# Cutting the warm-up matmuls at the head of an SSM-plus-dense kernel into chunks, two of them released by VectorE's layernorm sums

## The chip, the cores and the metric

The kernel runs on one core of one Trainium2 chip. The metric is the device time in microseconds (us). The profile follows one execution; its span (first to last instruction) is about 1.4 us shorter than the time that is counted. Engines: PE is TensorE, PEld its weight loads, DVE VectorE, ACT ScalarE, POOL GpSimd, SP SyncE.

## The reference, cut to what matters

```python
xn = _layernorm(x)                              # x: 1 x 2048 x 1024, bf16
out = x + ssm(xn, Lambda, B, C, log_dt, Dskip) + mish(xn @ w1 + b1) @ w2
# ssm: Bu = xn @ B_bar; a scan over the 2048 positions; y = 2 Re(h @ C) + xn * Dskip
```

The kernel takes the 2048 positions in four blocks of 512. A block does the first dense product, the SSM projection, the scan on VectorE, and a tail that adds the second dense product and the output projection in PSUM (the memory, in banks, that the matmuls here write). All of it needs xn transposed. For the first block nothing is there to hide that behind: this stretch, from the start to the first matmul on real weights, is the *head*.

## The kernel before

A helper records every operation with the tiles it reads and writes, and works out from them what it must wait for. An operation that writes a bank waits for that bank's last writer, also if that was on the same engine. The head:

```python
def keep_busy(n):                         # n matmuls of the identity with itself, result unused
    for i in range(n):
        PE.mm(lambda e: e.matmul(ps[:, 3, 0:P], lhsT=ident[:], rhs=ident[:], start=True, stop=True),
              reads=[b_ident], writes=[b_ps[3]], first=i == 0, last=i == n - 1)

keep_busy(44)
aop(... AF.Sqrt ...)                      # ScalarE: loads its table early (at 2.43 us, 1.28 us long)
PE.op(lambda e: e.transpose(ps16(2)[:, 0:NST], st[:, :], ident[0:NST, 0:NST]), ...)   # parameters
keep_busy(12)
for q in range(2):                        # layernorm of rows 0..255, 128 at a time
    first_sums_v(q, 0); first_sums_v(q, 1); first_var_v(q)      # VectorE -> mv[q]
    first_sqrt(q)                                               # ScalarE
first_apply(0)                            # VectorE: xn[0]
first_transpose(0)                        # TensorE: 8 transposes
keep_busy(4)
first_apply(1); first_transpose(1)
keep_busy(4)
first_copy(0, VE, 0, 4); first_copy(1, VE, 0, 4)                # PSUM -> xnT
first_copy(0, AC, 4, NK); first_copy(1, AC, 4, NK)
... # layernorm of rows 256..511
for f in range(NSPLIT):
    first_half(f, 0)                      # the first matmuls on real weights
```

The kernel gives each engine its operations in the order in which they stand here. The identity matmuls compute nothing that is used: they are there so that TensorE's clock is full when the real matmuls begin.

## Time and profile before

| | us |
|---|---|
| first three runs | 624.6, 622.09, 622.07 |
| span of the profiled execution | 620.41 |
| first matmul on real weights starts | 8.76 |
| from there to the end | 611.65 |
| full clock granted (clock record) | 6.50 |

The page of the kernel before, its busy shares and the chain that ended last by engine:

```profile
PE 613.4 (99%) x2905; PEld 287.6 (46%) x2961; DVE 465.6 (75%) x687; ACT 244.7 (39%) x158; POOL 49.9 (8%) x47
...
PE 96%; ACT 2%; DVE 1%; issue 1%; POOL 0%; DVEq 0%; POOLq 0%
```

TensorE bounds the kernel. The change touches only the head, so there the question is what holds up the first real matmul. The chain of waits of the first 24 us (start in us, length in us, what):

```profile
1.42 4.87 PE ps L462 x44
6.29 0.15 PE ps L467
6.44 0.82 PE ps L462 x12
7.26 0.45 PE ps L383 x8
7.71 0.22 PE ps L462 x4
7.93 0.24 PE ps L383 x4
8.17 0.02 issue
8.19 0.42 DVE xnT L396
8.62 0.13 DVE par L486
8.75 0.02 issue
8.76 2.78 PE ps L502 x24
```

L462 is the identity matmuls, L467 the parameter transpose, L383 the transposes of xn, L502 the real matmuls. The identity matmuls are *on* the chain: TensorE gets through them only a little after VectorE has the first xn ready. That is in the timeline (start, length, instruction), two lines from VectorE and one from TensorE:

```profile
6.04 0.21 DVE L351 BATCH_NORM_AGGREGATE mv<-stats 128x2 f32<-128x12 f32 x1
6.31 0.55 DVE L371 TENSOR_SCALAR xn<-xx,mv,rs 128x1024 bf16<-128x1024 bf16 x1
...
7.10 0.61 PE L383 MATMUL ps<-ident,xn 128*128 128x128 bf16 x8
```

xn is ready at 6.86 us, and the first transpose starts at 7.10.

The clock can be counted. These are windows of the same profile (stretch, its length, busy time of PE and the matmuls that began in it, granted clock, DMA share, GB/s):

```profile
5.00:6.00 1.00, 1.00 (x13) 1.00 1.14 343
7.00:8.00 1.00, 1.00 (x22) 1.00 0.98 309
```

The busy time is the same and the count isn't: start to start it is 106.7 ns at first and 55.8 ns later. (The column of the granted clock shows 1.00 in both, since there is no record before the first grant; the spacing has to be read instead.) The clock record of this trace grants 1.00 from 6.50 us, 5.1 us after TensorE's first matmul, for 614.399 us, and 0.50 after that, behind the last instruction. Below, W is the moment of full clock, and *half clock* is the state in which identity matmuls start 106.7 ns apart.

### The profile page before, as it was taken

The page shows a single profiled execution, that of the slowest core. Times are in us where ns is not written, and L with a number is a line of the kernel's source. Part 1 is how long each engine was busy: PE and PEld are TensorE (multiplying, and loading weights), DVE is VectorE, ACT ScalarE, POOL GpSimd, SP SyncE. Part 2 cuts the span into 40 slices and gives each one's busy share as a digit, 9 for nine tenths or more (in the row PEclk, how much of TensorE's full clock was granted, in tenths as well). Part 3 has the DMA queues.
Part 4 walks back from the last instruction along what each step waited for, and adds up shares of the span by engine and source line. Part 5 has one row for each costly group of instructions (what it writes and reads, how often), then busy time and mean ns, then how long its engine had stood idle before and what let it go on. Part 6 is the DMA issues. An engine that isn't in the chain of part 4 may idle for free.

```text
span 620.4 us, 7332 instructions
## 1 busy us (share of the span) xinstructions
PE 613.4 (99%) x2905; PEld 287.6 (46%) x2961; DVE 465.6 (75%) x687; ACT 244.7 (39%) x158; POOL 49.9 (8%) x47
## 2 busy tenths in 40 slices
PE   8999999999999999999999999999999999999998
PEld 8544444444444444444444444444444444444443
DVE  6899999999467599998147659999624856999603
ACT  5679995441079940000009992000001999000000
POOL 1998000000100000000010000000000000000000
PEclk9999999999999999999999999999999999999999
DMA  9999967740464301763065420285204542033001
GB/s 261 244 292 277 204 132 206 202 136 0 157 182 141 132 1 36 220 186 103 17 189 165 140 100 1 92 215 163 75 35 136 167 139 69 1 128 111 1 0 69
DMA packets 124332, 79.41 MB, mean 128 GB/s; under 512 B 48906, under 2 KB 106762, under 8 KB 124298
## 3 DMA queue, kind: packets, MB, share of 16 engines
q1 hardware_dynamic: 120800, 71.58, 42.4%
q10 hardware_dynamic: 2538, 4.21, 1.9%
q0 software_dynamic: 960, 3.15, 1.6%
q8 instruction: 24, 0.39, 0.3%
q14 instruction: 10, 0.08, 0.0%
HBM read 63.19 MB, written 4.19 MB: 109 GB/s over the span
## 4 chain that ended last, share of the span: by engine, by line
PE 96%; ACT 2%; DVE 1%; issue 1%; POOL 0%; DVEq 0%; POOLq 0%
PE ps L721 49%; PE ps L644 26%; PE ps L664 18%; PE ps L502 2%; PE ps L462 1%; ACT act L624 1%; ACT act L622 1%; ACT act L623 1%; DVE hb L651 0%; DVE act L629 0%; PE ps L383 0%; ACT L623 0%; DVE xx L436 0%; DVE xx L758 0%; DVE mt L434 0%
## 5 line engine op out<-in xcount | busy, mean ns | idle before, releaser
L721 PE MATMUL ps<-ring,act 128*128 128x512 bf16 x880 | 193.2, 379 | 0.8
L644 PE MATMUL ps<-xnT,ring 128*128 128x512 bf16 x832 | 182.7, 379 | 0.8
L622 ACT ACTIVATE act<-hb 128x3584 bf16<-128x3584 bf16 x16 | 50.9, 3183 | 244.2 <-DVE hb L651 243.7
L721 PEld LDWEIGHTS ps<-ring,act 128*128 128x128 bf16 x896 | 87.6, 98 | 105.8 <-DVE mt L669 0.3
L644 PEld LDWEIGHTS ps<-xnT,ring 128*128 128x128 bf16 x848 | 83.0, 98 | 99.8
L651 DVE TENSOR_SCALAR hb<-ps,par 128x512 bf16<-128x512 f32 x112 | 82.7, 747 | 55.1 <-PE ps L644 53.8
L664 PE MATMUL ps<-xnT,BT 128*128 128x512 bf16 x500 | 110.5, 379 | 0.6
L721 PE MATMUL ps<-CT,hT 128*128 128x512 bf16 x500 | 110.5, 379 | 0.6
L669 DVE TENSOR_TENSOR mt<-ps,tab 128x1024 bf16<-128x1024 f32 x64 | 75.3, 1219 | 13.3 <-PE ps L664 11.7
L664 PEld LDWEIGHTS ps<-xnT,BT 128*128 128x128 bf16 x512 | 50.1, 98 | 60.4
L721 PEld LDWEIGHTS ps<-CT,hT 128*128 128x128 bf16 x512 | 50.1, 98 | 60.4
L758 DVE TENSOR_TENSOR xx<-ps,xx 128x1024 bf16<-128x1024 f32 (+1 forms) x17 | 19.5, 1160 | 70.2 <-PE ps L721 70.1
L687 DVE TENSOR_TENSOR_SCAN hT<-cs,qi,hT 128x512 bf16<-128x512 f32 x48 | 58.9, 1268 | 0.0
L624 ACT ACTIVATE act<-act 128x3584 bf16<-128x3584 bf16 x16 | 51.0, 3190 | 0.2
L623 ACT ACTIVATE act<-act 128x3584 bf16<-128x3584 bf16 x16 | 51.0, 3190 | 0.2
L692 DVE TENSOR_TENSOR mt<-hT,tab 128x1024 bf16<-128x1024 bf16 x64 | 41.4, 688 | 1.1
L629 DVE TENSOR_TENSOR act<-act,hb 128x3584 bf16<-128x3584 bf16 x16 | 32.3, 2018 | 1.3 <-ACT act L624 1.3
L287 POOL DMA_DIRECT2D xx<-in_A_x_dram x12 | 6.7, 559 | 253.1 <-DVE xx L758 248.6
L598 ACT ACTIVATE ct<-CT,cs 128x512 f32<-128x512 bf16 x16 | 11.5, 718 | 28.8 <-DVE CT L600 24.5
L623 ACT ACT_TABLE_LOAD x16 | 20.5, 1283 | 0.3
L624 ACT ACT_TABLE_LOAD x16 | 20.5, 1283 | 0.3
L687 DVE TENSOR_TENSOR_SCAN hT<-cs,hT 128x512 bf16<-128x512 f32 x16 | 18.7, 1208 | 0.0
(78 smaller groups left out, 277.2 us busy)
## 6 DMA issues: line engine op xcount, KB each, us to landing
ring<-in_B_w_dram SPq DMA_DIRECT2D x112, 512.0 KB, 3.9
out_dram<-xx ACTq DMA_DIRECT2D x15, 256.0 KB, 2.1
xx<-in_A_x_dram POOLq DMA_DIRECT2D x12, 256.0 KB, 4.5
xx<-in_A_x_dram SPq DMA_DIRECT2D x3, 256.0 KB, 4.8
xx<-in_A_x_dram SPq DMA_DIRECT2D x2, 128.0 KB, 2.2
dsk<-in_A_Dskip_dram SPq DMA_DIRECT2D x1, 256.0 KB, 7.0
out_dram<-xx ACTq DMA_DIRECT2D x2, 128.0 KB, 1.7
xnT<-xn SPq DMA_TRANSPOSE x12, 4.5
```

Source lines behind the costliest of these rows:

```text
L622: aop(lambda e: e.activation(a, hs, AF.Exp), reads=[b_hb[g % 2]], writes=[b_act[g]])
L623: aop(lambda e: e.activation(a, a, AF.Ln, bias=1.0), reads=[b_act[g]], writes=[b_act[g]])
L624: aop(lambda e: e.activation(a, a, AF.Tanh), reads=[b_act[g]], writes=[b_act[g]])
L629: vop(lambda e: e.tensor_tensor(a, a, hs, op=ALU.mult), reads=[b_act[g], b_hb[g % 2]], writes=[b_act[g]])
L644: PE.mm(lambda e, k=k: e.matmul(ps[:, bank, :], lhsT=wt[:, k, fi * P:(fi + 1) * P], rhs=xnT[:, k, :], start=k == 0, stop=k == NK - 1), rea ...
L651: vop(lambda e: e.tensor_scalar(hb[:, hs, :], ps[:, bank, :], b1(f), None, op0=ALU.add), reads=[b_ps[bank], b_par], writes=[b_hbf[hs]])
L664: PE.mm(lambda e, j=j, ci=ci, k=k, bank=bank: e.matmul(ps[:, bank + ci, :], lhsT=BT[:, ci, j, k, :], rhs=xnT[:, k, :], start=k == 0, stop= ...
L669: vop(lambda e, s=s, u=u, j=j: e.tensor_tensor(mt[:, s, :, :], u, tab[:, s, j, :].unsqueeze(1).to_broadcast([P, 2, TB]), op=ALU.mult), rea ...
L687: vop(lambda e, ci=ci, init=init: e.tensor_tensor_scan(out=hT[:, ci, j, :], data0=cj("r", j).to_broadcast([P, TB]), data1=hT[:, ci, j, :], ...
L692: vop(lambda e, s=s: e.tensor_tensor(mt[:, s, :, :], hT[:, :, j, :], tab[:, s, j, :].unsqueeze(1).to_broadcast([P, 2, TB]), op=ALU.mult), ...
L721: PE.mm(lambda e: e.matmul(ps[:, u, :], lhsT=lhsT, rhs=rhs, start=st_, stop=last), reads=reads, writes=[b_ps[u]], first=st_, last=last)
L758: vop(lambda e: e.tensor_tensor(xr, src, xr, op=ALU.add), reads=b_src + [b_x], writes=[b_x])
```

## The change

Its intent is that TensorE has work in every part of the head: the identity matmuls come in chunks, two of which are released by VectorE's finished sums.

```diff
-    def keep_busy(n):
+    def keep_busy(n, until=()):
         for i in range(n):
             PE.mm(lambda e: e.matmul(ps[:, 3, 0:P], lhsT=ident[:], rhs=ident[:], start=True, stop=True),
-                  reads=[b_ident], writes=[b_ps[3]], first=i == 0, last=i == n - 1)
-
-    keep_busy(44)
+                  reads=[b_ident, *until] if i == 0 else [b_ident], writes=[b_ps[3]], first=i == 0, last=i == n - 1)
+
+    keep_busy(30)
     aop(...)
-    PE.op(... transpose of the parameters ...)
-    keep_busy(12)
     for q in range(2):
         first_sums_v(q, 0)
         first_sums_v(q, 1)
         first_var_v(q)
         first_sqrt(q)
+        keep_busy(20 - 6 * q, until=[b_mv[q]])
+    PE.op(... transpose of the parameters ...)
     first_apply(0)
     first_transpose(0)
-    keep_busy(4)
+    keep_busy(3)
     first_apply(1)
     first_transpose(1)
-    keep_busy(4)
+    keep_busy(5)
```

Ahead of the first transpose of xn that makes 64 identity matmuls in three chunks (30, 20, 14) instead of 56 in two. The order on every other engine is the same.

More of the change, by code (lines that the diff above doesn't have):

```diff
@@ L457, in smalls @@
             reads=[b_cs[in0]], writes=[b_cs[out_]])
-    def keep_busy(n):
+    def keep_busy(n, until=()):
         for i in range(n):
             PE.mm(lambda e: e.matmul(ps[:, 3, 0:P], lhsT=ident[:], rhs=ident[:], start=True, stop=True),
-                  reads=[b_ident], writes=[b_ps[3]], first=i == 0, last=i == n - 1)
-    keep_busy(44)
+                  reads=[b_ident, *until] if i == 0 else [b_ident], writes=[b_ps[3]], first=i == 0, last=i == n - 1)
+    keep_busy(30)
     aop(lambda e: e.activation(rs[:, :, 3], kon[:, 2:3].to_broadcast([P, NQ]), AF.Sqrt), reads=[b_kon], writes=b_rs)
-    PE.op(lambda e: e.transpose(ps16(2)[:, 0:NST], st[:, :], ident[0:NST, 0:NST]),
-          reads=[b_st, b_ident], writes=[b_ps[2]])
-    keep_busy(12)
     for q in range(2):
@@ L474, in build_kernel @@
         first_sqrt(q)
+        keep_busy(20 - 6 * q, until=[b_mv[q]])
+    PE.op(lambda e: e.transpose(ps16(2)[:, 0:NST], st[:, :], ident[0:NST, 0:NST]),
+          reads=[b_st, b_ident], writes=[b_ps[2]])
     first_apply(0)
     first_transpose(0)
-    keep_busy(4)
+    keep_busy(3)
     first_apply(1)
     first_transpose(1)
-    keep_busy(4)
+    keep_busy(5)
     first_copy(0, VE, 0, 4)
```

## The prediction

> **What bounds the kernel.** TensorE: the page gives PE 99% of the span, and the chain that ended last is 96% PE. Only the head (0 to 8.8 us) changes. There PE runs only identity matmuls, one small transpose and the first layernorm's transposes. The chain over the first 24 us goes: 44 identity matmuls (4.87 us), small transpose, 12 identity matmuls, 8 transposes, 4 identity matmuls, 4 transposes, VectorE's copy of xnT (0.42), then the first real matmuls at 8.76 us. After that the waits of PE show only 0.2 us, so what the head gains or loses should reach the end one for one.
>
> **The clock.** In the trace the identity matmuls start 106.7 ns apart up to 6.4 us and 55.8 ns apart after it; the clock record says full speed from 6.50 us. [...]PE started at 1.41 us, full clock came 5.1 us later. So the moment of full clock (W) should vary from run to run[...]. I suspect that in the 624.6 run it came late[...]; the other two (622.07, 622.09) had it early.
>
> **What the change does.** Ahead of the first data transpose, 44+12 identity matmuls become 30+20+14, 8 more; the small transpose moves behind them. Each chunk writes the same bank, so it waits for the last one to end: in the trace a chunk follows that end by 0.09 us, a bubble of about 0.25 us; there is one more. The releases cost little: VectorE's first sums end at 4.69 us, the second at 6.25 (timeline); 30 cold matmuls end at 4.79, so chunk two starts at about 4.9 us, released as much by its own engine. The later chunks (4 and 4 to 3 and 5) are worth 0.06 us. VectorE's and ScalarE's order doesn't change.
>
> **Sum.** First xn is ready at 6.86 us, first transpose before at 7.10. After, with full clock at 6.5 us: chunk two's last matmul starts at 6.72, chunk three runs 7.03 to 7.8, first transpose 7.87, second group 8.49 (7.77 before), first real matmul about 9.5 instead of 8.76: +0.7 us. [...]The change buys dense PE work[...], and the 624.6 kind of run should vanish. The usual run gets slightly slower, the rare bad one better.
>
> Predicted median 622.6 us, 80% range 621.8 to 623.9; faster by over 2%: 0.005, within 2%: 0.99, slower: 0.005.
>
> **What would show it.** Right: first real matmul at 8.9 to 9.8 us; chunk three ends after xn0 is ready, so that the first data transpose waits on PE's own order; no PE idle over 0.3 us from 1.4 us to the transposes; everything after the same, shifted. Wrong: first real matmul at or before 8.76 us; chunk two or three waiting visibly for VectorE; a later wait that absorbs the shift.
>
> **What would make it wrong.** [...] If the 624.6 run has another cause (DMA, for one), after shows such runs too. [...]

The marked cuts took out what no trace of this case shows: the range expected for W, the reason supposed for a late clock, and what was built on these. From the sum they took the term for W at 8.2 us and that for W near 5 us. What is left of it came to +0.7 us at W = 6.5 us (first real matmul at about 9.5 us instead of 8.76); the forecast of 622.6 us was made with the cut terms. "Cold" means at half clock.

## The result, and the profile after

| | before | after |
|---|---|---|
| median of the two kernels' runs beside each other (6 each) | 622.26 | 622.75 |
| lowest, highest | 622.07, 624.6 | 622.11, 623.12 |
| span of the profiled execution | 620.41 | 621.11 |
| first transpose of xn starts | 7.10 | 7.83 |
| first real matmul starts | 8.76 | 9.45 |
| from there to the end | 611.65 | 611.66 |

The ratio of after to before is 1.0002 (95% interval 0.9986 to 1.0017): the same. A ratio is the mean time of one kernel's fast runs over that of the other's of the same rounds, so it isn't quite the ratio of the medians. Here the one run of 624.6 lifts the mean of before.

The chain of waits of the kernel after, first 24 us:

```profile
1.42 3.39 PE ps L462 x30
4.81 0.14 issue
4.95 1.75 PE ps L462 x20
6.69 0.14 issue
6.83 0.94 PE ps L462 x14
7.77 0.13 PE ps L473
7.90 0.55 PE ps L383 x8
...
9.45 2.78 PE ps L502 x24
```

(L473 is now the parameter transpose.) The head is still TensorE's own order, and longer. There are two "issue" pieces of 0.14 us that before had not: a chunk that waits for the chunk ahead of it. What the weight loads of the second and the third chunk waited for, and xn, from the timeline:

```profile
4.92 1.59 PEld L462 LDWEIGHTS ps<-ident 128*128 128x128 bf16 x20 [0.39 <-DVE mv L351]
...
6.31 0.55 DVE L371 TENSOR_SCALAR xn<-xx,mv,rs 128x1024 bf16<-128x1024 bf16 x1
6.80 0.80 PEld L462 LDWEIGHTS ps<-ident 128*128 128x128 bf16 x14 [0.29 <-issue]
...
7.83 0.62 PE L383 MATMUL ps<-ident,xn 128*128 128x128 bf16 x8
```

The profile puts the first wait down to VectorE's sums, but those ended at 4.72 us, while the last matmul of the first chunk ended at 4.80: both ended within 0.1 us of each other, and who was last is a matter of modelled ends. xn is ready at 6.86 us as before, and TensorE comes to it 0.97 us later. Everything behind the first real matmul takes 611.66 us, as before (611.65), so the head's 0.69 us reaches the end whole.

In this execution the spacing turns from 106.7 to 55.8 ns at about 5.9 us. (The trace has no clock record in this execution, though the spacing shows the change.) So the two profiles do not have the same W, and the difference of 0.69 us is not yet the cost of the change at equal clock.

### The profile page after: what moved, and what is told of

Same layout as the page of the kernel before. It is cut to its first block, busy times and chain, and to the rows that moved or that the text cites. A ratio compares the mean times of both kernels' runs of the same rounds, so it can differ in the third digit from the quotient of the medians.

```text
span 621.1 us, 7406 instructions
## 1 busy us (share of the span) xinstructions
PE 616.8 (99%) x2969; PEld 287.8 (46%) x2969; DVE 465.7 (75%) x687; ACT 244.8 (39%) x158; POOL 49.9 (8%) x47
## 4 chain that ended last, share of the span: by engine, by line
PE 99%; DVE 0%; POOL 0%; issue 0%; POOLq 0%
PE ps L721 49%; PE ps L644 29%; PE ps L664 18%; PE ps L502 2%; PE ps L462 1%; PE ps L383 0%; DVE xx L758 0%; DVE xnT L396 0%; POOL ident L330 0%; POOL ident L329 0%; DVE par L486 0%; PE ps L473 0%; POOL kon L333 0%; POOLq L844 0%
```

## The experiments

Theory: the head's time is TensorE's own order, that is the number of identity matmuls, the bubbles between chunks, and W, which varies from run to run. The prediction also supposed that the kernel's few runs near 624.6 are runs in which full clock came late. Rivals: VectorE's release or the place of the parameter transpose costs the time; the slow runs come from late data. Whether transposes bring full clock as matmuls do was open. The twelve kernels ran each on one chip beside the kernel before; all results were correct.

### Which part of the change costs what

**a_again, a_third: the changed kernel again**, without an edit.

> The changed kernel unaltered, for more samples beside the kernel before. Theory (the extra time is TensorE's own order: more identity matmuls and one more wait between chunks, and the moment of full clock varies from run to run): median 0.3 to 0.8 us above the kernel before, all runs between 622.0 and 623.6, while the kernel before has most runs at 622.0 to 622.5 and now and then one near 624.6. Rival (no difference at all, the first comparison was noise): medians within 0.15 us.

> The changed kernel once more, for the spread: if the change had done away with late runs, none of its runs would lie over 623.6. One of twelve so far did (624.57), as two of 26 of the kernel before did (624.6, 624.98). Expected: median 622.3 to 622.9, and runs over 623.6 about as rare as in the kernel before.

Measured: a_again 622.41 median (622.20 to 624.57) against 622.13 for before; ratio 1.0006 (0.9987 to 1.0025). a_third 622.66 (622.12 to 622.92) against 622.38; ratio 0.9993 (0.9977 to 1.0010). In all three comparisons the median of after is 0.3 to 0.5 us higher, and in all three the means can't be told apart. Neither side of a_again's expectation is met as it stands: 0.28 us lies between the theory's 0.3 and the rival's 0.15, and one run of 624.57 was not to be. What the change costs is therefore read from the traces.

**a_onechunk: one chunk of 64**

```diff
-    keep_busy(30)
+    keep_busy(64)
-        keep_busy(20 - 6 * q, until=[b_mv[q]])
```

> The changed kernel with its 64 identity matmuls in one chunk: same count, no wait between chunks. Theory: the two bubbles (4.49 to 4.95 and 6.46 to 6.83 us in the trace after, about 0.35 and 0.31 us more than a matmul slot) vanish, but at the same count the first real matmul only moves from 9.45 to about 8.8 to 9.3 us, depending on the moment of full clock; time 0.3 to 0.6 us under the changed kernel. Rival (the bubbles don't matter, only the count does): as the changed kernel.

Measured: 622.43 median, ratio to before 1.0005 (0.9988 to 1.0021). The expected 0.3 to 0.6 us under the changed kernel doesn't show in the times (a_again had 622.41). The runs can't resolve it, the trace can: W was 6.11 us by its clock record and the first real matmul came at 9.06 us.

**a_fewer: three chunks, 56 in all**

```diff
-        keep_busy(20 - 6 * q, until=[b_mv[q]])
+        keep_busy(20 - 14 * q, until=[b_mv[q]])
```

> The changed kernel with 30, 20 and 6 identity matmuls, 56 ahead of the first transpose as in the kernel before. Theory (the extra time is the 8 added matmuls at 56 ns and the bubbles): first real matmul 0.45 us sooner than in the changed kernel at the same moment of full clock, so 9.0 us at 5.9 us; time 0.4 us under the changed kernel, 0.1 to 0.3 us over the kernel before. Rival (the place of the small transpose or the release by VectorE costs the time): as the changed kernel.

Measured: 622.17 median, before 622.17; ratio 0.9999 (0.9986 to 1.0011). In its trace W was 6.11 us too, first real matmul 9.08 us.

**a_nowait: three chunks without the release by VectorE**

```diff
-        keep_busy(20 - 6 * q, until=[b_mv[q]])
+        keep_busy(20 - 6 * q)
```

> The changed kernel with the three chunks, but not released by VectorE's sums. Theory: the release costs next to nothing since each chunk waits for the end of the one before anyway; the bubbles shrink by 0.06 us each at most (the second wait's issue), time within 0.15 us of the changed kernel. Rival (the wait for VectorE is what moves the head): first real matmul 0.3 us or more earlier.

Measured: 622.62 median, ratio 1.0003 (0.9988 to 1.0018). Here full clock came late, at 7.44 us, and the first real matmul at 9.95. The first bubble (last matmul of one chunk to first of the next) was 0.375 us instead of 0.460 with the release. (The second was 0.374; it fell in half clock here and in full clock in the trace after, so these two can't be compared.)

To compare these at one clock I use the traces. A microsecond of half clock costs 1 - 55.8/106.7 = 0.48 us of identity matmuls. At W = 5.9 us there is, from the experiment b_tr below, a head in before's order, with transposes in place of the identity matmuls:

```profile
6.39 0.55 DVE L371 TENSOR_SCALAR xn<-xx,mv,rs 128x1024 bf16<-128x1024 bf16 x1
...
6.99 0.62 PE L383 MATMUL ps<-ident,xn 128*128 128x128 bf16 x8
...
8.66 2.78 PE L502 MATMUL ps<-xnT,ring 128*128 128x256 bf16 x24 [0.16 <-DVE par L486]
```

Its first real matmul comes at 8.66 us. The changed kernel at 5.9 us has 9.45: **0.79 us more at equal clock**. The first real matmuls of a_fewer and of a_onechunk:

```profile
9.08 1.14 PE L502 MATMUL ps<-xnT,ring 128*128 128x256 bf16 x9
9.06 1.14 PE L501 MATMUL ps<-xnT,ring 128*128 128x256 bf16 x9
```

The parts of the 0.79 us, by traces at W = 6.11 (where the changed kernel would be at 9.54, an estimate from the 0.48):

- 8 more matmuls: 9.54 - 9.08 = 0.46 us (8 x 55.8 ns is 0.45).
- the two bubbles: 9.54 - 9.06 = 0.48 us. In the trace after they are 0.460 and 0.368 us where a matmul slot is 0.107 and 0.056: 0.35 us at half clock, which is worth 0.19 at full, and 0.31 at full.
- one identity matmul less between the transposes: -0.06 us.
- b_tr waits for xn, which is ready at 6.94 us: its last identity transpose starts at 6.86, the first transpose of xn at 6.99, 0.13 us later instead of 0.056: -0.08 us.

That makes 0.80. The parameter transpose costs the same in both places: from the matmul before it to the one after it are 0.28 us in b_tr and in the trace after. In before's order that time also covers the second chunk's wait for the first; in the changed kernel both waits come on top of it.

The release is a small part of the bubbles in these runs (0.085 us on the first). The rival that it alone moves the head by 0.3 us falls for the usual run. But a_third shows how it can: in its profiled execution the second slice of x landed late, VectorE's second sums ended at 7.17 us, and the third chunk stood waiting for them; xn was ready at 7.78, and the first transpose came only at 8.24, behind the 14 matmuls. First real matmul: 9.86 us. (By its own order TensorE would have come to xn at 7.83, as in the trace after, so the release cost some 0.4 us there; this is an estimate.) When data is late, the release puts 14 useless matmuls behind the late sums.

### When full clock comes

**b_tr: the kernel before with transposes in place of identity matmuls**

```diff
-            PE.mm(lambda e: e.matmul(ps[:, 3, 0:P], lhsT=ident[:], rhs=ident[:], start=True, stop=True),
+            PE.mm(lambda e: e.transpose(ps16(3)[:, 0:P], ident[:], ident[:]),
```

> The kernel before with every identity matmul turned into a transpose of the identity matrix (same count, same bank, same order). Theory A [...]: the clock stays low through the head, spacing 106.7 ns in all of it[...]: 3 to 5 us slower than before. Theory B (transposes count like matmuls): [...]time as before.

Measured: 622.76 median of 4 runs (621.79 to 623.2), ratio 1.0004 (0.9985 to 1.0023). The clock record says full speed from 5.92 us. Windows of its profile (busy time of PE, PEld, DVE, ACT, POOL, with counts; clock; DMA share; GB/s):

```profile
4.00:5.00 1.00, 1.00 (x12) 1.00 (x10) 0.97 (x3) 0.17 (x1) 0.00 (x0) 1.00 1.06 311
6.00:7.00 1.00, 1.00 (x17) 0.78 (x14) 0.93 (x5) 0.29 (x1) 0.00 (x0) 1.00 1.07 357
```

12 in a microsecond turn into 17 with two gaps among them, with nothing but transposes on TensorE up to then. Theory A falls: **transposes, as this kernel issues them, brought full clock as matmuls do** (5.92 us here, 5.9 to 7.44 with matmuls in before, after, a_onechunk, a_fewer and a_nowait). The trace lists them as MATMUL and doesn't show a mode of their own.

**b_duty: before's first chunk cut into seven chunks of 4, the second to 4** (so 32 instead of 56)

```diff
-    keep_busy(44)
+    for _ in range(7):
+        keep_busy(4)
-    keep_busy(12)
+    keep_busy(4)
```

> The kernel before with its 44 identity matmuls cut into 7 chunks of 4, each of which waits for the end of the one before, and the 12 into 4: TensorE starts a matmul in only about six tenths of the time up to 6.5 us. Theory A (bubbles between chunks don't put off full clock, so the changed kernel's two don't either): [...]time as before. Theory B[...], first real matmuls 213 ns apart, 0.8 to 3 us slower than before.

Measured: 624.16 median of 4 runs (622.68 to 625.8); ratio to before 1.0017 (0.9989 to 1.0045), so the times alone don't settle it. The trace does. Full clock came at 13.22 us. Windows of PE in its profile:

```profile
4.00:6.00 2.00, 1.82 (x14) 1.00 1.00 283
10.00:12.00 2.00, 2.00 (x12) 1.00 1.17 288
14.00:15.00 1.00, 1.00 (x16) 1.00 1.20 291
```

At 10 to 12 us the real matmuls go 6 to a microsecond (213 ns apart), half of what they do at full clock (109 ns). So theory B, that the bubbles go with a late full clock, holds up to the first xn: until 6.4 us TensorE's only holes were bubbles (0.37 us from start to start) and those around the parameter transpose, and the clock stayed at half. Then came a hole of 0.92 us, in which TensorE, out of matmuls, waited for xn. What each of the two did to the 13.22 us is not shown. The page hides the bubbles: PE counts as 91% busy at 4 to 6 us, because the modelled end of a matmul lies 311 ns behind its start while the next can start after 107.

**b_late and b_none: TensorE idle for longer**

b_late, with `until` as in the changed kernel:

```diff
-    keep_busy(44)
-    keep_busy(12)
+    keep_busy(16, until=[b_mv[0]])      # ahead of first_transpose(0)
```

b_none:

```diff
-    keep_busy(44)
-    keep_busy(12)
-    keep_busy(4)                        # both of these
```

The theory of both was that full clock comes later where TensorE stood idle.

> The kernel before with its first 56 identity matmuls replaced by 16 that are released by VectorE's first sums at about 4.7 us: TensorE idles until then. Theory [...]: 0.5 to 2.3 us slower than before, a wide spread, the slowest near the 624.6 to 625.0 that few runs of the others show. Rival (what makes those few runs slow is not a late clock but late data): time as before, the first real matmul at 8.6 to 8.8 us at full clock.

> The kernel before without any identity matmul. Theory: transposes from 6.95 us at 106.7 ns, first real matmul at about 9.0 us at half speed (about 213 ns apart instead of 109)[...]: 1.2 to 3 us slower than before. Rival: as before, since VectorE's chain alone sets the head.

Measured: b_late 622.98 median (622.81 to 624.04), ratio 1.0012 (0.9999 to 1.0024); b_none 623.11 (622.77 to 624.88), ratio 1.0024 (1.0009 to 1.0040). In the traces full clock came at 10.51 and 10.55 us, first real matmul at 9.51 and 9.09, and the rest took 612.07 and 612.26 us instead of 611.65. Two of b_none's five runs took 624.73 and 624.88; they have no trace. The theory of idle time and late clock holds, but at the low end of what was expected of b_late and below it for b_none. Look at the size: *all* the identity matmuls together are worth 0.24%, and an execution of these two kernels with full clock 4 us late has a time of 622.8 to 623, not 624.6. That doesn't clear the clock, though. These kernels have few or no identity matmuls for a late clock to draw out. In b_duty, with full clock 6.7 us later than in the kernel before, the first real matmul came 1.2 us later, everything from 58 us on came 2.7 us later, and the execution took 624.55 us. Some 0.5 us of that is xn, ready at 7.38 us instead of 6.86; the rest is half clock. So a clock that comes 6.7 us late does make a run of that kind.

With the starts in the traces one can work out how long TensorE stood idle before full clock (gaps from start to start, each less one slot of 107 ns):

| run | TensorE's first matmul | full clock | between | idle in it |
|---|---|---|---|---|
| before | 1.41 | 6.50 | 5.1 | 0.2 |
| b_less (below) | 1.42 | 6.48 | 5.1 | 0.2 |
| after | 1.42 | 5.9 | 4.5 | 0.35 |
| b_tr | 1.42 | 5.92 | 4.5 | none |
| a_onechunk | 1.42 | 6.11 | 4.7 | none |
| a_fewer | 1.41 | 6.11 | 4.7 | 0.35 |
| a_nowait | 1.42 | 7.44 | 6.0 | 0.54 |
| b_none (from its first transpose of xn) | 7.02 | 10.55 | 3.5 | 0.39 |
| b_duty | 1.42 | 13.22 | 11.8 | 2.7 |

Where the holes add up to 0.54 us at most, full clock came 3.5 to 6.0 us after the first matmul; with 2.7 us of them it took 11.8. (b_late, whose identity matmuls waited for the first sums, ready at 4.78 us, had full clock at 10.51; its holes are not summed up here.) No run in the table lies between, so how much idle time is too much is not shown, nor why the dense starts differ by 2.5 us among themselves. In its trace the kernel before had 0.2 us of holes and its full clock 2.3 us ahead of the first real matmul: that left the change next to nothing to fill. The longest hole alone doesn't tell a late clock: b_none had one of 0.39 us and full clock 3.5 us after its first transpose of xn, while b_duty up to 6.4 us had none over 0.27 us and was still at half clock, 5.0 us after its start. And in the traced execution of b_less the clock was full from 6.48 us, TensorE then idled for 1.3 us in all up to 9.9 us (0.76 us of it in one wait for xn), and the clock stayed full (8 transposes of xn took 0.62 us, as in before).

### What the slow runs are, and whether anything beats both

**b_less: before with fewer identity matmuls (40 and 6)**

```diff
-    keep_busy(44)
+    keep_busy(40)
-    keep_busy(12)
+    keep_busy(6)
```

> The kernel before with 40 and 6 identity matmuls ahead of the first transpose instead of 44 and 12: few enough to be done before xn is ready (about 6.9 us) even if all of them run at half speed. Theory (with a late full clock the surplus identity matmuls themselves hold up the first transpose; with an early one they cost nothing): first transpose at 6.9 to 7.1 us whatever the moment of full clock, first real matmul at 8.55 to 8.7 us if full clock comes by 6.9 us; runs between 621.6 and 622.6, median 0.1 to 0.3 us under the kernel before. Rival (the shorter run leaves TensorE idle for up to 1 us[...]): some or most runs at 623 or more.

Measured: 623.82 median; runs 622.11 to 624.36, five of six over 623.6. Ratio 1.0011 (0.9993 to 1.0029). By the numbers this looks like the rival, that idle time puts off full clock. The trace, from an execution of 624.25 us, says otherwise: full clock at 6.48 us, first real matmul at 9.13 (VectorE's sums began late, behind data), and 613.72 us from there to the end. Most of the two extra microseconds is far behind the head: b_less lags the kernel before by 0.37 us at the first real matmul, by 0.78 at the first matmul of the tail (86.7 us) and by 2.43 at 136.7 us and ever after. PE's waits over the whole of b_less:

```profile
PE ps L721 <- DVE mt L669: 1.2, 1, 1.2
PE ps L383 <- DVE xn L371: 0.8, 1, 0.8
```

The first one is new and lies in that stretch; the second is in the head. Its place in b_less's timeline, with what delayed VectorE:

```profile
36.56 2.35 POOL L287 DMA_DIRECT2D xx<-in_A_x_dram  x4
...
44.69 1.42 DVE L405 BATCH_NORM_STATS2 stats<-xx 128x6 f32<-128x512 bf16 x2 [1.27 <-DMA xx<-in_A_x_dram]
...
93.96 3.41 PE L721 MATMUL ps<-ring,act 128*128 128x512 bf16 x15 [1.21 <-DVE mt L669]
```

And the same loads and sums in the timeline of the kernel before:

```profile
36.03 2.34 POOL L287 DMA_DIRECT2D xx<-in_A_x_dram  x4
...
42.80 1.41 DVE L405 BATCH_NORM_STATS2 stats<-xx 128x6 f32<-128x512 bf16 x2
```

In b_less the second block's rows took 8.2 us from issue to landing (median of the four loads; 4.9 in before). VectorE stood idle for 1.27 us and took that delay to the end of the projection: the last eviction there ended at 93.91 us, where TensorE's tail wanted those banks at 92.6. In before that eviction ends at 91.45 us, and TensorE, by its spacing, reaches those banks at about 91.5: there is next to no slack, so a late load in the fortieth microsecond becomes a wait of TensorE in the ninetieth. The kernel before had four runs of 624.0 to 624.4. So this slow run is a matter of late data, not of the clock. That the other runs near 624.5 (before: 624.6 and 624.98; after: 624.57) have the same cause is not shown: they have no trace, and b_duty's 624.55 came for the most part from the clock. Even within b_less one run points elsewhere: that of 623.96 us has a mean granted clock of 0.997 on record, where every other fast run has 1.0. By estimate that is 3.1 to 4.4 us at a clock of 0.50 (0.25 to 0.35% of 622.5 us, doubled), worth 1.5 to 2.1 us (x 0.48). Where in the run it lay is not known, so for that run the rival isn't ruled out. Nor is it shown that fewer identity matmuls don't bring such runs about; one kernel with five of six slow runs (before had four of eleven) leaves that open.

**b_early and b_early_less: an earlier start**, on a tile that VectorE fills itself, instead of waiting for GpSimd's identity:

```diff
+    warm = sb("warm", [P, P], bf16)
+    vop(lambda e: e.memset(warm[:], 1.0), writes=[b_warm])
-    keep_busy(44)          # all of them on warm, not ident
+    keep_busy(48)          # b_early;       b_early_less: 42
     ...
     keep_busy(12)          # b_early as it was;    b_early_less: 6
```

> The kernel before, but its identity matmuls read a tile that VectorE fills with ones at the very start, 48 in the first chunk instead of 44, so that TensorE starts about 0.6 us sooner than the 1.41 us at which GpSimd's identity matrix is ready. Theory [...]: first transpose at 7.0 to 7.2 us, time 621.6 to 622.5 in every run, median equal to or up to 0.3 us under the kernel before. Rival (the start of TensorE's work doesn't matter within the head): same distribution as before.

> The earlier start on a tile of ones, now with 42 and 6 identity matmuls. Theory: TensorE starts at 1.1 us, first transpose at 6.9 to 7.1 us, runs 621.6 to 622.5. If the granted clock of 0.754 of the first profile with this tile comes again, the tile of ones (or the earlier start) has to do with it; if it doesn't, that was a state of the chip at that moment.

Measured: b_early's four timed runs were 622.02, 623.01, 624.31 and 622.66 (ratio 1.0010, 0.9995 to 1.0025), three of them over the expected 622.5. TensorE started at 1.11 us, only 0.3 us sooner: VectorE's own first instruction came no earlier than 0.89. Its profiled execution:

```profile
core 0: 811.7 us, clock 0.754
```

The clock rose at 5.92 us to a recorded 0.752 and stayed there to the end. It is left out of every comparison. It didn't come again in the six runs of b_early_less, and I have no cause for it.

b_early_less: 622.18 median (621.78 to 623.74) against 622.38, ratio 0.9991 (0.9973 to 1.0009). Its first real matmul came at 8.68 us, but then TensorE waited at 10.96 for weights:

```profile
10.96 1.05 PE L505 MATMUL ps<-xnT,ring 128*128 128x256 bf16 x8 [0.38 <-DMA ring<-in_B_w_dram]
```

It isn't the early head alone that brings this wait: b_tr, with its first real matmul at 8.66 us, had none there, and b_less, with 9.13, had one at 11.12. So it goes with when the loads land in an execution. No version here beats both kernels clearly.

## Why the prediction was right or wrong, point by point

- **The time.** Predicted 622.6 (621.8 to 623.9), measured 622.75; "within 2%" is right.
- **What bounds the head: TensorE's own order.** Right. In the profile after, TensorE reached xn 0.97 us after it was ready, and the first real matmul at 9.45 us lies in the predicted 8.9 to 9.8.
- **One for one to the end.** Right: 611.65 us from the first real matmul before, 611.66 after.
- **The size, +0.7 us at W = 6.5.** The measured +0.69 us matches by two errors that cancel. Full clock in the profile after came at 5.9 us, 0.6 us sooner than the +0.7 supposes, which makes it about +0.4 (an estimate: 0.6 x 0.48 is 0.29). The mis-sized term is "a bubble of about 0.25 us": the bubbles measured 0.35 and 0.31 us over a slot, and there were two more, not one, since before's only bubble lay behind the parameter transpose. At equal W the change costs 0.79 us.
- **"No PE idle over 0.3 us".** Narrowly wrong for the same reason.
- **The releases cost little.** Right for the usual run (0.085 us on the first), wrong for an execution with late data (a_third), where the third chunk waited visibly for VectorE.
- **W varies from run to run.** Right: 5.9 to 7.4 us in the profiled executions with a dense start.
- **"the 624.6 kind of run should vanish".** This step failed. The reason that it rested on was not shown. Transposes brought full clock too (b_tr, 5.92 us), and in its trace before's head had 0.2 us of holes and full clock at 6.50 us, so that the change had next to nothing to add. Such runs didn't vanish either: the changed kernel had one in 18 (624.57), before six in 37, too few to call a difference. What makes them stays open: of the two slow executions with a trace, b_less's was late data, b_duty's for the most part a clock 6.7 us late, and no slow run of before or after has one.

## What to carry to other kernels

In this head warm-up matmuls should end before the first real operand is ready, and come in one piece: each chunk that waited for its predecessor left a hole of a third of a microsecond, and each matmul past the operand's arrival delayed everything behind it. Both show in the traces and are too small for the times. Before filling holes, work out from the starts of the matmuls whether the holes matter at all: here removing all the warm-up cost 0.24%, and the kernel before already got its full clock at 6.50 us, ahead of its first real matmul at 8.76. If rare slow runs are the motive, get a trace of one first; here one that was caught came from a load issued at 36 us, another (b_duty) for the most part from the clock.
